# Key-value sums of a linear-attention block: one 128-column matmul for four heads, or four 32-column tiles

## The chip, the core and the metric

The kernel runs on one core of one Trainium2 chip. The metric is the device time of one execution in microseconds (us). Before the change it is 559.03 us, the median of three runs (558.52 to 559.60). All line numbers are those of the kernel before.

## The reference, cut to what matters

A block of linear attention with 32 heads of 32 channels is followed by an MLP over the tokens; x is 2048 tokens by 1024 channels, in bfloat16. The part at issue is `kv` and `z`:

```python
qkv = (layernorm(x) @ wqkv)                  # split in q, k, v; H = 32 heads, Dh = 32
phi = lambda t: where(t > 0, t + 1, exp(t)) + 1e-6
pq, pk = phi(q), phi(k)
kv  = einsum("bhsd,bhse->bhde", pk, v)       # 32x32 per head, summed over the 2048 tokens
z   = einsum("bhsd->bhd", pk)                # 32 per head
num = einsum("bhqd,bhde->bhqe", pq, kv)
den = einsum("bhqd,bhd->bhq", pq, z)[..., None] + 1e-6
o   = num / den
h   = x + o.reshape(B, S, D) @ wo
h2  = h + mlp_over_tokens(layernorm(layernorm(h)))   # S x F and F x S weights, F = 3584
```

Of each head's keys and values only the head's own 32x32 block of sums is wanted, and beside it the plain sum of its keys.

## The kernel before, in words

The 2048 tokens are 16 tiles of 128 (NS = 16), the 1024 channels 8 groups of 128 (ND = 8), so one group holds HB = 4 heads of DH = 32. The execution has three stages: up to about 143 us the layer norm, the projections to q, k and v and the key-value sums; up to about 230 us the folding of the sums into the output weights, the denominators and the attention's output; then the MLP over tokens, until the end at 557.7 us.

In the first stage keys and values of two token tiles at a time are computed by seven block products of 512 columns (class `Run`, lines 966 and following, with `KRun` and `VRun`); some of the queries (`q_unit`, line 1298; `QRun`, line 1103) are computed among them. Nearly every operation is pinned, so the order in the program text is the order on each engine. `run_step` writes that order out: of each run the products p1, p6, p2, p5, p7 and, inside the next run's step, p3 and p4.

The results go to two rings of four buffers each. `pks` holds phi of the keys of a token tile, 128 x 1024 bfloat16. `vaugs` holds the values, as 8 groups of 129 columns: 128 values and a one (line 814). The ones are filled in at the start (line 816). The values are written by ACT (line 903 for the first two tiles, line 1034 after that) and by DVE (line 1037, which adds two PSUM results).

`kv_accum(i)` (line 914) adds one token tile to the sums. For each group j of four heads it does one matmul on the full array: 128 tokens by the 128 key columns of the group are the stationary operand, the group's 129 value columns are the moving one, and 128 x 129 numbers are added in PSUM (line 917). All 16 cross products of four key heads with four value heads are computed, of which the four on the diagonal are wanted; column 129 is the sum of the keys. A PSUM bank holds three such groups (KPB = 3), so the eight groups take NKB = 3 banks (line 1281). The banks are cleared by DVE (line 1293), and the matmuls only ever accumulate (start=False). `kv_accum` is called for two token tiles at a time, eight times in all: after the first two products of the first value run (line 1322), behind p5 of the value runs (lines 1355, 1356), and at the end of the stage (lines 1377, 1378).

Behind the last call stand three more query units on TensorE (line 1379). Meanwhile DVE takes the sums out of PSUM: it multiplies each bank by a mask that holds 1/S on the four diagonal blocks and 0 elsewhere (`maskbd`, lines 105 to 110) into `kvbd` (line 1385), and spreads the key sums into `zz` (line 1391). `kv_transpose` (line 1418) then transposes kvbd on TensorE, and `den_mm` multiplies zz with the queries. `den_mm` is the one place where this kernel uses a part of the array: four matmuls of 32 stationary columns and 512 moving ones go to four column tiles (tile_position = (0, g * 32)) of one PSUM bank, for two sets of four groups.

Two other users are to be known: `warm_up` (line 98) does matmuls at the very start, among them two tiny ones whose operands are 128 x 6 and 128 x 2 float32; and `transpose_half` (line 1179) transposes in 128 x 128 blocks.

```python
        def kv_accum(i):                                  # line 914
            for j in range(ND):
                b, sl = divmod(j, KPB)
                pin(nc.tensor.matmul(
                    kv_ps[b][:, sl, :],
                    lhsT=pks[i % NPK][:, j * P:(j + 1) * P],
                    rhs=vaugs[i % NVA][:, j, :],
                    start=False, ...))
```

Of the kernel before, what the change touches and what calls it, by code (L numbers as in the profile page):

```python
# [10 lines left out]
P = 128  # L11
F32 = mybir.dt.float32
BF16 = mybir.dt.bfloat16
FP16 = mybir.dt.float16
ACT = mybir.ActivationFunctionType
ALU = mybir.AluOpType
# [5 lines left out]
DH = 32  # L22
BANK = 512
# [7 lines left out]
def kernel(  # L31
# [12 lines left out]
    nc = tc.nc  # L44
    x = A_x.flatten_outer_dims()
    o_dram = out.flatten_outer_dims()
    S, D = x.shape
    F = B_w1.shape[1]
    NS, ND, NF = S // P, D // P, F // P
    CW = min(BANK, D)  # L50
# [7 lines left out]
    JB = CW // P  # L58
    HB = P // DH
    QR = P // 4  # L60
    assert ND == 8 and 3 * HB <= QR
    KPB = BANK // (P + 1)
    NKB = (ND + KPB - 1) // KPB

    const = ctx.enter_context(tc.tile_pool(name="const", bufs=1))
    actx_psum = ExitStack()
# [18 lines left out]
    pin = tc.keep_in_program_order  # L85
# [16 lines left out]
        for t in range(n):  # L102
            mm(warm[:, 0:P], warm[:, 0:BANK])

    maskbd = const.tile([P, P], F32)
    nc.vector.memset(maskbd[:], 0.0)
    m4 = const.tile([P, HB], F32)
    nc.vector.memset(m4[:], 0.0)
    for q in range(HB):
        nc.vector.memset(maskbd[q * DH:(q + 1) * DH, q * DH:(q + 1) * DH], 1.0 / S)  # L110
        nc.vector.memset(m4[q * DH:(q + 1) * DH, q:q + 1], 1.0)
    eps_ln = const.tile([P, 1], F32)
    nc.vector.memset(eps_ln[:], LN_EPS)
# [70 lines left out]
    def phi_parts(dst, src, n, pool, view=lambda t: t, lean=False):  # L184
        e_sb = pool.tile([P, n], BF16, tag="phi_e", name="e_sb")
        r_sb = None if lean else pool.tile([P, n], BF16, tag="phi_r", name="r_sb")

        def act():
            pin(nc.scalar.activation(e_sb[:], src, ACT.Exp))  # L189
            if not lean:  # L190
                pin(nc.scalar.activation(r_sb[:], src, ACT.Relu))

        def dve():
            pin(nc.vector.tensor_scalar(e_sb[:], e_sb[:], 1.0, PHI_EPS, ALU.min, ALU.add))  # L194
            if lean:
                pin(nc.vector.scalar_tensor_tensor(dst, view(src), 0.0, view(e_sb[:]), ALU.max, ALU.add))
            else:
                pin(nc.vector.tensor_tensor(dst, view(e_sb[:]), view(r_sb[:]), ALU.add))

        return act, dve  # L200

    def phi_evac(dst, src, n, pool):
        for part in phi_parts(dst, src, n, pool):
            part()
# [222 lines left out]
    class Mixer1(Product7):  # L427
# [5 lines left out]
        def evac(self, fh, dh, ps, a=0, b=CW):  # L433
            ft = 2 * self.p + fh
            act.activation(
                (gE if fh == 0 else gO)[:, self.p, dh * CW + a:dh * CW + b],
                ps[:, a:b], ACT.Gelu_apprx_tanh, bias=b1_sb[:, ft:ft + 1], scale=1.0,
            )
# [74 lines left out]
    class Quad:  # L513
# [85 lines left out]
        def run2(self, rest, nxt, load, sums, cut):  # L599
# [38 lines left out]
            def third():  # L638
                self.in3 = Inner2(sts, 3, self.mov3, "i", self.add_to(e), None)
                shared(sts[0])  # L640
                evac(0, 0, self.t1)()
                self.in3.sums(slice(0, 2))

            self.interleave(in2, self.pieces(lambda st: st.p7_fill), {
                "b": every(lambda: sts[0].asum(3), sums[3]), "2": lambda: sts[1].asum(3),
                "7": lambda: load("p7"), "third": third,
                "end": lambda: self.late.append(evac(1, 0, self.t1)),
            }, (("7", None),))
            shared(sts[1])
# [9 lines left out]
            def begin_next():  # L659
                if nxt is not None:  # L660
                    nxt.in1 = nxt.inner(1)
                    nxt.in1.sums(slice(0, 2))
                evac(0, 1, e)()
# [119 lines left out]
    with ExitStack() as actx:  # L783
# [14 lines left out]
        kvbd = pqpool.tile([P, ND, P], BF16)  # L798
        zz = pqpool.tile([P, ND, QR + HB], BF16)
# [10 lines left out]
        with ExitStack() as a1:  # L810
            a1w = a1.enter_context(tc.tile_pool(name="a1w", bufs=1))
            wkv = a1w.tile([P, ND, 2 * D], BF16)
            NVA, NPK = 4, 4
            vaugs = [a1w.tile([P, ND, P + 1], BF16, name=f"vaug{t}") for t in range(NVA)]
            for t in range(NVA):
                nc.vector.memset(vaugs[t][:, :, P:P + 1], 1.0)
            pks = [a1w.tile([P, D], BF16, name=f"pk{t}") for t in range(NPK)]
            tv = [
                t.bitcast(FP16).rearrange("p (k c) -> p k c", c=CW)
# [59 lines left out]
            def ln_finish(i):  # L879
                xn, _, _, scale, norm, _, _ = ln.pop(i)  # L880
                for op in scale():
                    pin(op)
                pin(norm(slice(0, D)))
                nc.sync.dma_start_transpose(out=xnT[:, :, i * P:(i + 1) * P], in_=xn[:])
# [13 lines left out]
            def proj_evac(pp, i, c):  # L898
                if c < NDC:
                    phi_evac(pks[i % NPK][:, c * CW:(c + 1) * CW], pp[:, 0:CW], CW, a2k)  # L900
                else:
                    c2 = c - NDC
                    pin(nc.scalar.activation(
                        vaugs[i % NVA][:, c2 * JB:(c2 + 1) * JB, 0:P],
                        pp[:, 0:CW].rearrange("p (j e) -> p j e", e=P),
                        ACT.Copy,
                    ))

            def proj_unit(i, c, hold=None):
                pp = acc_tile()  # L910
                proj_mm(pp, i, c, range(ND), hold)
                proj_evac(pp, i, c)

            def kv_accum(i):
                for j in range(ND):
                    b, sl = divmod(j, KPB)
                    pin(nc.tensor.matmul(  # L917
                        kv_ps[b][:, sl, :],
                        lhsT=pks[i % NPK][:, j * P:(j + 1) * P],
                        rhs=vaugs[i % NVA][:, j, :],  # L920
                        start=False,
                        stop=(i == NS - 1),
                        skip_group_check=True,
                    ))

            hk2 = ND // 2

# [98 lines left out]
            class VRun(Run):  # L1026
# [1 line left out]
                    super().__init__(q, vmov)  # L1028

                def dst(self, h, c):  # L1030
                    return vaugs[(2 * self.q + h) % NVA][:, c * JB:(c + 1) * JB, 0:P]

                def evac(self, h, ps):
                    pin(nc.scalar.activation(self.dst(h, 0), ps[:].rearrange("p (j e) -> p j e", e=P), ACT.Copy))

                def add(self, h, ps):
                    pin(nc.vector.tensor_tensor(
                        self.dst(h, 1),
                        ps[:].rearrange("p (j e) -> p j e", e=P),
                        self.E[:].rearrange("p (j e) -> p j e", e=P),  # L1040
                        ALU.add,
                    ))

            class KRun(Run):
# [233 lines left out]
            less_acc()  # L1278
            vps = a1.enter_context(tc.tile_pool(name="vps", bufs=1, space=PSUM))
            kvp = a1.enter_context(tc.tile_pool(name="kvp", bufs=1, space=PSUM))  # L1280
            kv_ps = [kvp.tile([P, KPB, P + 1], F32, name=f"kvps{b}") for b in range(NKB)]
            proj_unit(0, NDC, pin)
            ln_finish(G0)
            w_sums(vmov, slice(0, 2))
# [4 lines left out]
            w_sums(vmov, slice(2, 4))  # L1289
            proj_unit(1, NDC + 1, pin)  # L1290
            ln_finish(G0 + 1)
            for b in range(NKB):
                nc.vector.memset(kv_ps[b][:], 0.0)

            def q_unit(u, j):
                qp = acc_tile()
# [23 lines left out]
            v1.p1()  # L1320
            q_fill()
            kv_accum(0)
            kv_accum(1)
            v1.p6()
            v1.p2()
# [11 lines left out]
            for q in range(2, NVP):  # L1337
# [3 lines left out]
                for n in runs:  # L1341
                    kind = type(n).__name__[0]
                    i = {"K": 2 * q + 3, "V": 2 * q + 4}.get(kind, NS)
                    if q == 5 and kind == "Q":
                        i = NS - 1 if n.half == 1 else NS
                    elif q == 6 and kind == "K":
                        i = NS
# [5 lines left out]
                    def after5():  # L1353
                        if kind == "V":
                            kv_accum(2 * q - 2)
                            kv_accum(2 * q - 1)
                        if i < NS:
                            ln_finish(i)
                            load_next(i + 2)
# [20 lines left out]
                q_fill()  # L1380
            nc.vector.memset(zz[:, :, 0:3 * HB], 0.0)
            nc.vector.memset(zz[:, :, 3 * HB:], float(S))
            for b in range(NKB):
                j0, n = b * KPB, min(KPB, ND - b * KPB)
                nc.vector.tensor_tensor(
                    kvbd[:, j0:j0 + n, :],
                    kv_ps[b][:, 0:n, 0:P],
                    maskbd[:].unsqueeze(1).to_broadcast([P, n, P]),
                    ALU.mult,
                )  # L1390
                nc.vector.tensor_tensor(
                    zz[:, j0:j0 + n, HB:2 * HB],
                    kv_ps[b][:, 0:n, P:P + 1].to_broadcast([P, n, HB]),
                    m4[:].unsqueeze(1).to_broadcast([P, n, HB]),
                    ALU.mult,
                )

        more_acc(3)
        warmctx.close()
# [441 lines left out]
```

## Time and profile before

| what | value |
|---|---|
| median of 3 runs | 559.03 us |
| span of the profiled execution | 557.7 us |
| TensorE busy in the span | 550.7 us (99%) |
| DVE busy | 443.8 us (80%) |
| ACT busy | 288.8 us (52%) |
| TensorE clock granted | 1.00 |
| matmuls of line 917 (128 x 129) | 128, 221 ns each |
| their weight loads (128 x 128) | 128, 98 ns each |
| first and last start of them | 33.2 and 137.6 us |

The span goes from the first to the last instruction of the one profiled execution. The profile has no other time for that execution; its span is 1.3 us under the median of the runs. Matmuls overlap: the record of one lasts longer than the distance to the next, so the distance between starts is the cost of a matmul in a row of them, and a busy TensorE is not TensorE at its peak. In the rows of the profile PE is TensorE's matmuls, PEld its weight loads, a row in order of time has its start, the time from its first start to its last end, the engine, the line, the operation, the tile that is written and those that are read, the shape, and the count. The chain that ended last is followed back from the last instruction: at each step to what released it or to the instruction ahead of it on its engine.

### The profile page before, as it was taken

The page shows a single profiled execution, that of the slowest core. Times are in us where ns is not written, and L with a number is a line of the kernel's source. Part 1 is how long each engine was busy: PE and PEld are TensorE (multiplying, and loading weights), DVE is VectorE, ACT ScalarE, POOL GpSimd, SP SyncE. Part 2 cuts the span into 40 slices and gives each one's busy share as a digit, 9 for nine tenths or more (in the row PEclk, how much of TensorE's full clock was granted, in tenths as well). Part 3 has the DMA queues.
Part 4 walks back from the last instruction along what each step waited for, and adds up shares of the span by engine and source line. Part 5 has one row for each costly group of instructions (what it writes and reads, how often), then busy time and mean ns, then how long its engine had stood idle before and what let it go on. Part 6 is the DMA issues. An engine that isn't in the chain of part 4 may idle for free.

```text
span 557.7 us, 8915 instructions
## 1 busy us (share of the span) xinstructions
PE 550.7 (99%) x3370; PEld 320.4 (57%) x3387; DVE 443.8 (80%) x858; ACT 288.8 (52%) x614; POOL 26.2 (5%) x36
## 2 busy tenths in 40 slices
PE   8999999999999999999999999999999999999997
PEld 3444446645444444456766767666444667667665
DVE  6898888754488688889989789887996879749747
ACT  5747678665776877646556465464210412413311
POOL 1000000000000000000000000000003103103111
PEclk9999999999999999999999999999999999999999
DMA  8933341202966961102250440413769659849434
GB/s 297 308 76 76 80 89 22 39 0 72 317 155 192 316 196 75 76 0 90 64 152 4 148 133 21 150 43 91 202 204 237 190 137 242 209 126 240 94 106 75
DMA packets 83931, 74.51 MB, mean 134 GB/s; under 512 B 15650, under 2 KB 76336, under 8 KB 83888
## 3 DMA queue, kind: packets, MB, share of 16 engines
q1 hardware_dynamic: 79504, 69.87, 42.0%
q0 software_dynamic: 4096, 3.68, 5.0%
q8 instruction: 26, 0.43, 0.3%
q10 hardware_dynamic: 288, 0.39, 0.2%
q14 instruction: 17, 0.14, 0.1%
HBM read 59.12 MB, written 11.67 MB: 127 GB/s over the span
## 4 chain that ended last, share of the span: by engine, by line
PE 91%; DMA 4%; DVE 2%; ACT 1%; SPq 1%; issue 0%; DVEq 0%; ACTq 0%
PE psI L234 23%; PE psC L234 14%; PE acc_t L234 14%; PE psB L234 8%; PE psC L966 4%; PE psB L966 4%; PE psA L966 4%; PE acc_t L888 3%; PE acc_t L1298 2%; PE psB L346 2%; PE psA L346 2%; PE psE L966 2%; PE psC L346 2%; DMA wq<-in_B_w_dram 2%; DMA wkv<-in_A_wqkv_dram 1%; PE kvps L917 1%
## 5 line engine op out<-in xcount | busy, mean ns | idle before, releaser
L234 PEld LDWEIGHTS <-is 128*128 128x128 f16 x736 | 71.8, 98 | 31.3 <-DVE is L234 0.4
L234 PEld LDWEIGHTS <-sa 128*128 128x128 f16 x606 | 59.2, 98 | 27.5 <-issue 0.3
L234 PEld LDWEIGHTS <-wq 128*128 128x128 bf16 (+1 forms) x496 | 48.5, 98 | 28.1 <-issue 1.2
L234 PE MATMUL acc_t<-wo_sb,pqT 128*128 128x512 f16 x256 | 55.6, 379 | 0.0
L491 POOL DMA_DIRECT2D out_dram<-wq x28 | 24.3, 927 | 519.6 <-ACT wq L494 487.7
L234 PEld LDWEIGHTS <-pqT 128*128 128x128 bf16 x256 | 25.0, 98 | 30.5 <-issue 0.6
L234 DVE TENSOR_TENSOR t<-psI,t 128x256 f32<-128x256 f32 (+1 forms) x45 | 20.8, 475 | 22.2 <-PE psI L234 21.0
L194 DVE TENSOR_SCALAR e_sb<-e_sb 128x512 bf16<-128x512 bf16 x64 | 18.4, 287 | 21.8 <-ACT e_sb L189 21.6
L234 PE MATMUL psC<-gs,wq 128*128 128x512 f16 x140 | 34.1, 379 | 0.0
L966 PEld LDWEIGHTS <-xs 128*128 128x128 f16 x208 | 20.1, 98 | 22.1 <-DVE xs L955 0.6
L234 PE MATMUL psC<-hT,sa 128*128 128x512 f16 x112 | 31.2, 379 | 0.0
L234 PE MATMUL psI<-hi,is 128*128 128x256 f16 x200 | 30.0, 273 | 0.0
L234 PE MATMUL psB<-hT,sa 128*128 128x512 f16 x112 | 29.7, 379 | 0.0
L234 PE MATMUL acc_t<-xnT,wq_sb 128*128 128x512 bf16 x125 | 29.3, 379 | 0.3
L189 ACT ACTIVATE e_sb<-acc_t 128x512 bf16<-128x512 f32 x32 | 19.1, 598 | 18.6 <-PE acc_t L1298 10.0
L234 DVE BATCH_NORM_STATS2 hst<-acc_t 128x6 f32<-128x512 f32 x32 | 21.4, 691 | 9.1 <-ACT h_bf L234 8.9
L966 PE MATMUL psA<-wkv,xnT 128*128 128x512 bf16 x98 | 26.2, 379 | 0.3
L966 PEld LDWEIGHTS <-xnT 128*128 128x128 bf16 x156 | 15.2, 98 | 18.1 <-issue 0.2
L234 PE MATMUL psC<-hT,wq 128*128 128x512 f16 x96 | 24.6, 379 | 0.0
L234 ACT CAST h_bf<-acc_t 128x512 bf16<-128x512 f32 x32 | 18.4, 582 | 12.0 <-PE acc_t L234 12.0
L234 DVE TENSOR_TENSOR e<-psI,es 128x256 f32<-128x256 f32 x20 | 8.5, 424 | 19.9 <-PE psI L234 19.9
L234 ACT COPY psI<-psI 128x256 f32<-128x256 f32 x50 | 18.0, 360 | 11.7 <-PE psI L234 9.8
(246 smaller groups left out, 1131.6 us busy)
## 6 DMA issues: line engine op xcount, KB each, us to landing
wq<-in_B_w_dram SPq DMA_DIRECT2D x14, 1024.0 KB, 7.9
wq<-in_B_w_dram SPq DMA_DIRECT2D x12, 896.0 KB, 7.6
gs<-parked SPq DMA_DIRECT2D x9, 896.0 KB, 4.7
shared_sb<-rd_dram SPq DMA_DIRECT2D x32, 128.0 KB, 3.9
out_dram<-h_bf SPq DMA_DIRECT2D x16, 256.0 KB, 2.0
x_sb<-in_A_x_dram SPq DMA_DIRECT2D x14, 256.0 KB, 3.0
w2o<-in_B_w_dram SPq DMA_DIRECT2D x4, 896.0 KB, 11.3
out_dram<-wq POOLq DMA_DIRECT2D x28, 128.0 KB, 4.6
```

The costliest lines, as they stand in the source:

```text
L189: pin(nc.scalar.activation(e_sb[:], src, ACT.Exp))
L194: pin(nc.vector.tensor_scalar(e_sb[:], e_sb[:], 1.0, PHI_EPS, ALU.min, ALU.add))
L234: return (lambda *a, **kw: pin(op(*a, **kw))) if self.always or getattr(Held, self.key) else op
L346: pe.matmul(ps[:, cols], lhsT=lhs[:, k, :], rhs=mv(k)[:, cols], start=(start and k == 0), stop=(k == self.nk - 1), skip_group_check=True,)
L491: nc.gpsimd.dma_start(to, ot[:, a:b], accum_op=ALU.add)
L888: mm = nc.tensor.matmul(pp[:, 0:CW], lhsT=xnT[:, kt, i * P:(i + 1) * P], rhs=wkv[:, kt, c * CW:(c + 1) * CW], start=(kt == 0), stop=(kt == ...
L917: pin(nc.tensor.matmul(kv_ps[b][:, sl, :], lhsT=pks[i % NPK][:, j * P:(j + 1) * P], rhs=vaugs[i % NVA][:, j, :], start=False, stop=(i == N ...
L966: pin(nc.tensor.matmul(ps[:], lhsT=lhs[:, k, :], rhs=rhs[:, k, :], start=(start and k == 0), stop=(k == hk2 - 1), skip_group_check=True,))
L1298: nc.tensor.matmul(qp[:, 0:SW], lhsT=wq_sb[:, kt, j * P:(j + 1) * P], rhs=xnT[:, kt, u * SW:(u + 1) * SW], start=(kt == 0), stop=(kt == ND ...
```

## The change

The sums are accumulated per head. For each group of four heads four matmuls are issued, head q of the group on column tile q: 128 tokens by the head's 32 key columns are stationary, the head's own 32 value columns and its one are moving, and 32 x 33 numbers are added at PSUM partitions 32q to 32q + 31. The 8 x 33 columns fit into one bank. The value buffers are laid out by head, 32 groups of 33 columns. The mask goes; kvbd is filled with zeros once, near the start of the program, and at the end four DVE operations copy the diagonal blocks, scaled by 1/S.

```diff
-            vaugs = [a1w.tile([P, ND, P + 1], BF16, name=f"vaug{t}") for t in range(NVA)]
+            vaugs = [a1w.tile([P, ND * HB, DH + 1], BF16, name=f"vaug{t}") for t in range(NVA)]
             for t in range(NVA):
-                nc.vector.memset(vaugs[t][:, :, P:P + 1], 1.0)
+                nc.vector.memset(vaugs[t][:, :, DH:DH + 1], 1.0)
+
+            def heads(t, c):
+                return t[:, c * JB * HB:(c + 1) * JB * HB, 0:DH]
+
+            def by_head(t):
+                return t.rearrange("p (h e) -> p h e", e=DH)
...
             def kv_accum(i):
                 for j in range(ND):
-                    b, sl = divmod(j, KPB)
-                    pin(nc.tensor.matmul(
-                        kv_ps[b][:, sl, :],
-                        lhsT=pks[i % NPK][:, j * P:(j + 1) * P],
-                        rhs=vaugs[i % NVA][:, j, :],
-                        start=False,
-                        stop=(i == NS - 1),
-                        skip_group_check=True,
-                    ))
+                    for q in range(HB):
+                        h = j * HB + q
+                        pin(nc.tensor.matmul(
+                            kv_ps[q * DH:(q + 1) * DH, j, :],
+                            lhsT=pks[i % NPK][:, h * DH:(h + 1) * DH],
+                            rhs=vaugs[i % NVA][:, h, :],
+                            start=False,
+                            stop=(i == NS - 1),
+                            skip_group_check=True,
+                            tile_position=(0, q * DH),
+                        ))
...
                 def evac(self, h, ps):
-                    pin(nc.scalar.activation(self.dst(h, 0), ps[:].rearrange("p (j e) -> p j e", e=P), ACT.Copy))
+                    pin(nc.scalar.activation(self.dst(h, 0), by_head(ps[:]), ACT.Copy))
...
-            kv_ps = [kvp.tile([P, KPB, P + 1], F32, name=f"kvps{b}") for b in range(NKB)]
+            kv_ps = kvp.tile([P, ND, DH + 1], F32, name="kvps")
...
-            for b in range(NKB):
-                nc.vector.memset(kv_ps[b][:], 0.0)
+            nc.vector.memset(kv_ps[:], 0.0)
+            nc.vector.memset(kvbd[:], 0.0)
...
-            for b in range(NKB):
-                j0, n = b * KPB, min(KPB, ND - b * KPB)
-                nc.vector.tensor_tensor(
-                    kvbd[:, j0:j0 + n, :],
-                    kv_ps[b][:, 0:n, 0:P],
-                    maskbd[:].unsqueeze(1).to_broadcast([P, n, P]),
-                    ALU.mult,
-                )
-                nc.vector.tensor_tensor(
-                    zz[:, j0:j0 + n, HB:2 * HB],
-                    kv_ps[b][:, 0:n, P:P + 1].to_broadcast([P, n, HB]),
-                    m4[:].unsqueeze(1).to_broadcast([P, n, HB]),
-                    ALU.mult,
-                )
+            for q in range(HB):
+                own = slice(q * DH, (q + 1) * DH)
+                nc.vector.tensor_scalar(kvbd[own, :, own], kv_ps[own, :, 0:DH], 1.0 / S, None, ALU.mult)
+            nc.vector.tensor_tensor(
+                zz[:, :, HB:2 * HB],
+                kv_ps[:, :, DH:DH + 1].to_broadcast([P, ND, HB]),
+                m4[:].unsqueeze(1).to_broadcast([P, ND, HB]),
+                ALU.mult,
+            )
```

Not shown are the removal of `maskbd` and of KPB and NKB, and the same change of view in the other writers of the value buffers (lines 903 and 1037). The order of all other instructions on TensorE, ACT, SP and POOL is the same.

More of the change, by code (lines that the diff above doesn't have):

```diff
@@ L61 @@
     assert ND == 8 and 3 * HB <= QR
-    KPB = BANK // (P + 1)
-    NKB = (ND + KPB - 1) // KPB
+    assert ND * (DH + 1) <= BANK
     const = ctx.enter_context(tc.tile_pool(name="const", bufs=1))
@@ L103, in warm_up @@
             mm(warm[:, 0:P], warm[:, 0:BANK])
-    maskbd = const.tile([P, P], F32)
-    nc.vector.memset(maskbd[:], 0.0)
     m4 = const.tile([P, HB], F32)
@@ L109 @@
     for q in range(HB):
-        nc.vector.memset(maskbd[q * DH:(q + 1) * DH, q * DH:(q + 1) * DH], 1.0 / S)
         nc.vector.memset(m4[q * DH:(q + 1) * DH, q:q + 1], 1.0)
@@ L903, in proj_evac @@
                     pin(nc.scalar.activation(
-                        vaugs[i % NVA][:, c2 * JB:(c2 + 1) * JB, 0:P],
-                        pp[:, 0:CW].rearrange("p (j e) -> p j e", e=P),
+                        heads(vaugs[i % NVA], c2),
+                        by_head(pp[:, 0:CW]),
                         ACT.Copy,
@@ L1030, in dst @@
                 def dst(self, h, c):
-                    return vaugs[(2 * self.q + h) % NVA][:, c * JB:(c + 1) * JB, 0:P]
+                    return heads(vaugs[(2 * self.q + h) % NVA], c)
                 def evac(self, h, ps):
-                    pin(nc.scalar.activation(self.dst(h, 0), ps[:].rearrange("p (j e) -> p j e", e=P), ACT.Copy))
+                    pin(nc.scalar.activation(self.dst(h, 0), by_head(ps[:]), ACT.Copy))
                 def add(self, h, ps):
                     pin(nc.vector.tensor_tensor(
[L1038 to L1041, printed above, removed]
+                        self.dst(h, 1), by_head(ps[:]), by_head(self.E[:]), ALU.add,
                     ))
```

## The prediction

> **What bounds the kernel now.** I read the busy shares first, then the chain of waits, then the instructions in order of time around the lines that the change touches. TensorE is busy for 550.7 of 557.7 us. The two lines tell the limit before any detail: no other engine comes near, and DVE's 443.8 us is spread under TensorE.
>
> ```profile
> span 557.7 us, 8915 instructions
> PE 550.7 (99%) x3370; PEld 320.4 (57%) x3387; DVE 443.8 (80%) x858; ACT 288.8 (52%) x614; POOL 26.2 (5%) x36
> PE 91%; DMA 4%; DVE 2%; ACT 1%; SPq 1%; issue 0%; DVEq 0%; ACTq 0%
> ```
>
> The last line is the chain that ended last: 91% of it is TensorE, so what the change adds to or takes from TensorE's queue goes to the end of the kernel nearly one to one. The chain between 30 and 150 us holds the key-value sums eight times, each time as a block of 16 matmuls (two token tiles). Three of the eight pieces (start, length):
>
> ```profile
> 33.38 0.94 PE kvps L917 x16
> ...
> 52.53 0.94 PE kvps L917 x16
> ...
> 136.90 0.94 PE kvps L917 x16
> ```
>
> The same block in order of time, with its neighbours (start, from first start to last end):
>
> ```profile
> 51.94 0.59 PE L966 MATMUL psE<-wo_sb,xs 128*128 128x512 f16 x2
> 52.37 1.11 PE L917 MATMUL kvps<-vaug,pk 128*128 128x129 bf16 x16
> 53.31 0.59 PE L966 MATMUL psC<-wo_sb,xs 128*128 128x512 f16 x2
> ```
>
> One matmul's record lasts 221 ns but they overlap: the next work starts 53.31 - 52.37 = 0.94 us later, so the pace is 0.94/16 = 59 ns for a weight load and a matmul. No wait stands before or behind the block. Eight blocks are 8 x 0.945 = 7.56 us of chain: the whole stake of the change.
>
> **What the new form costs, by the nearest rows.** The trace has one matmul in the new shape's column width: the denominators on zz, 128 rows by 32 columns, 512 moving columns, four tiles side by side.
>
> ```profile
> 144.38 0.81 PE L234 MATMUL acc_t<-xnT,wq_sb 128*128 128x512 bf16 x3
> 145.13 0.62 PE L234 MATMUL den_ps<-pqT,zz 128*32 128x512 bf16 x8
> 145.67 0.61 PE L234 MATMUL acc_t<-xnT,wq_sb 128*128 128x512 bf16 x2
> ```
>
> Two things are in it. First, the tiles do run side by side: eight matmuls of 512 columns take 0.62 us from first start to last end, where eight on the full array at 216 ns apart would take 7 x 0.216 + 0.38 = 1.89 us. A window of 0.06 us shows four of them started within 0.40 - 0.39 = some 0.01 us, so 3 to 4 ns apart:
>
> ```profile
> 145.13 0.40 PE L234 MATMUL den_ps<-pqT,zz 128*32 128x512 bf16 x4
> ```
>
> Second, changing the tile width costs time. The last full-width matmul before starts at 144.38 + 0.81 - 0.38 = 144.81; the next start should come 0.216 later and comes 0.31 later: 0.095 lost. The last wave on the tiles starts at 145.13 + 0.62 - 0.38 = 145.37 and the next full-width one at 145.67, again 0.31 less 0.216, 0.095 lost; the one behind that starts 0.227 later, 0.01 lost. In all **0.20 us per block**, 8 x 0.20 = 1.6 us, that the blocks of before do not pay.
>
> The rest is 64 weight loads and 64 matmuls of 33 columns per block instead of 16 and 16. No row has a long run of such small ones, so I bound their pace from both sides. The low end: four at a time and limited by columns alone, 59 x 33/129 = 15 ns for each of 16 groups of four, 0.24 us. The high end: each pair keeps the 59 ns at which the pairs of before come, 64 x 59 = 3.78 us. In between lie the only tiny matmuls of the trace, 6 and 2 columns:
>
> ```profile
> 5.03 0.20 PE L98 MATMUL acc_t<-st 128*6 128x6 f32 x2
> 5.48 0.19 PE L98 MATMUL acc_t<-mv 128*2 128x2 f32 x2
> ```
>
> One lasts 173 and 166 ns, so the second starts 27 to 31 ns behind the first, though there is next to nothing to stream: a pair costs some 29 ns on one tile. The open question is whether 29 ns is what one tile needs (then four tiles share it) or what TensorE needs to bring up the next pair in a run longer than it has ready. The 3 to 4 ns of zz speak for the first, but they are bursts of 8 to 16 instructions that stood ready behind the change of width; here 128 follow each other. The trace never shows TensorE take more than 32 instructions at under 30 ns each (the block of 16 pairs: 0.945 us/32). I take 29 ns for each of the 64 pairs, as the nearest row in size, and keep both ends.
>
> Sum for a block: 64 x 0.029 + 0.20 - 0.945 = +1.11 us. All eight: +8.9 us.
>
> What a notes page makes of it, beside those rows: the Trainium skill, TensorE: Matmul & The Clock Gate, section "Wait — 56ns, not 53.3ns?", says that starts never come closer than about 25 ns however few the columns, and that a sequencer that decodes in firmware needs about 62 ns per matmul. By the first figure my sum would be 8 x (1.60 + 0.20 - 0.945) = +6.8 us, by the second 8 x (3.97 + 0.20 - 0.945) = +25.8 us, estimates from that page. The 27 to 31 ns agree with the first; the 3 to 4 ns between different column tiles do not, for a burst. [...]
>
> **The other edits, none on the path.**
> - Value buffers by head (18 ACT writes on lines 903 and 1034, 600 ns each; 14 DVE adds on line 1037, 685 ns): same counts, runs of 32 numbers instead of 128. No row shows runs of 32. I take no change; between a loss of nothing and double, it would be 10.8 us more of ACT and 9.6 us more of DVE, where between 30 and 140 us ACT is busy 76.4 and DVE 85.6 of 110. Each add has the next two runs' matmuls, over 5 us, before its value block is read. Without that cover the 9.6 us would be the price; I give it 3%.
> - The end of the sums (lines 1385, 1391): six DVE operations, 2 x 0.54 + 0.41 + 3 x 0.155 = 1.96 us from 137.77 to 139.68, become four of 32 partitions x 256 and one of 128 x 32. Nearest row 0.41 for 256 columns: 4 x 0.41 + 0.16 = 1.8 us. The transposes that read them start at 142.86; three query units of TensorE, 5.2 us, cover it. Value nothing, between -0.1 and +0.1; without cover that is also what it would cost.
> - Clearing: three fills of 0.38 us at 22.5 to 25.4 become one of 264 columns (0.26), and the filling of kvbd comes in at the start, about 0.5 us by the same row, for five mask fills that go (0.17 + 4 x 0.09). DVE there idles 1.12 us for the first tile of x, and TensorE waits for neither: nothing.
> - The freed two PSUM banks are given to nobody; the order of the other TensorE work, ACT's, SP's and POOL's is the same, and no DMA moves. The first matmul of the sums keeps its wait for the clearing; the last fill of before starts at 25.4, the first matmul at 33.2.
>
> **The rivals.**
> 1. *The tiles carry it: faster.* If groups of four come at 29 ns (or at 15), a block is 16 x 0.029 + 0.20 = 0.66 us (0.44): 0.28 (0.50) saved, eight times -2.2 (-4.0) us: 556.8 (555.0). For it: 3 to 4 ns between tiles in the zz row, TensorE's later weight loads already issued while the first wave runs. Against it: never seen over more than 16 instructions. It decides when a pair comes up in under (0.945 - 0.20)/64 = 11.6 ns.
> 2. *TensorE is fed no faster than now: slower still.* At 59 ns a pair: 8 x (3.78 + 0.20 - 0.945) = +24.3 us, 583.3. For it: no run in the trace is denser. Against it: 59 ns at 129 columns can be the columns alone.
> 3. *Neither: within 0.2% (1.1 us).* Part of a block stands ready while the 512-column matmuls before it run, the rest comes at the slow pace; with 11.6 ns on average the two cancel. A narrow band between my case and rival 1.
> 4. *The change does not do what it says*, because four tiles on one bank wait for each other: then each pair costs one tile's 29 ns, which is my number again. The zz row, also four tiles on one bank, speaks against it.
>
> **How the numbers follow.** The profiled execution's span is 557.7 us, the median of the three runs 559.03; I keep the 1.3 us between them and add my sum to the median: 559.0 + 8.9 = **567.9 us**. Chances: my case and everything slower 56% (of it 13% above 579, near rival 2), rival 3 8%, rival 1 36%, almost all of it between 555.0 and 557.9. The range takes in rival 1 and leaves the far end of rival 2 out: 555.0 to 579.0. The likeliest case's own range is 562 to 574 (20 to 40 ns a pair: 8 x (1.28 + 0.20 - 0.945) = +4.3 to 8 x (2.56 + 0.20 - 0.945) = +14.5). 0.2% is about what a measurement of this kernel can tell from no change.
>
> **What will show it.** In the changed profile the sums should be 512 matmuls of 128*32, 33 columns, in eight places; the length of such a place, from its first start to the next full-width start, is the whole answer: about 2.1 us if I am right, 0.44 to 0.67 if the tiles carry it, 4.0 for rival 2, 0.945 for no change. An equal gap of 0.31 us on both sides should show the change of width. DVE's and ACT's rows for vaug should stay at 685 and 600 ns; a longer one, and TensorE idle behind it, would make me wrong for another reason, and so would any gap in TensorE outside these eight places.

## The result, and the profile after

The changed kernel takes 557.3 us (median of 12 runs, 556.87 to 558.55) beside 558.63 us for the kernel before (12 runs): ratio 0.9976, 95% interval 0.9967 to 0.9984. Timed again later, beside other runs of the kernel before, it gave 0.9966 (0.9952 to 0.9979). So it is faster by some 1.3 to 1.9 us, where I had forecast 8.9 us slower. The time went the way of rival 1.

Page of the changed kernel, the lines that answer to those shown of before:

```profile
span 555.3 us, 9676 instructions
PE 548.3 (99%) x3754; PEld 316.7 (57%) x3771; DVE 443.6 (80%) x851; ACT 289.0 (52%) x614; POOL 26.2 (5%) x36
PE 95%; DMA 2%; ACT 1%; DVE 1%; issue 1%; ACTq 0%; DVEq 0%
```

TensorE still bounds the kernel and is busy 2.4 us less, as much as the span is shorter; DVE and ACT are where they were. A profiled execution's time lies 1.75 us above its span here (557.03 and 555.3 for this one), so the first profile of before, with 557.7, was of an execution of 559.4 us, and its span is 0.4 to 0.8 us too long to be set against a median.

The chain of waits between 30 and 150 us, three of the eight places of the sums (start, length):

```profile
33.15 0.59 PE kvps L920 x64
...
52.07 0.59 PE kvps L920 x64
...
135.55 0.60 PE kvps L920 x64
```

and one place in order of time with its neighbours:

```profile
51.04 1.03 PE L970 MATMUL psE<-wo_sb,xs 128*128 128x512 f16 x4
52.00 0.66 PE L920 MATMUL kvps<-vaug,pk 128*32 128x33 bf16 x64
52.59 1.04 PE L970 MATMUL psC<-wo_sb,xs 128*128 128x512 f16 x4
```

The last full-width matmul ahead starts at 51.04 + 1.03 - 0.38 = 51.69, and 0.216 is its own due; the next full-width one starts at 52.59. The place costs 0.69 us (0.68 by these rounded numbers, 0.690 in the trace at each of the eight), and the start behind that one comes 0.01 late: 0.70, where it cost 0.945. The 64 matmuls themselves start within 0.66 - 0.18 = 0.48 us; the other 0.21 to 0.22 are the two changes of width. Inside, the starts of groups of four lie 25 ns apart for about the first 36 matmuls and 33 ns apart from then on, which is 8.3 ns a pair, or 4.2 ns for each of the 8 instructions of a group. On average a pair takes 7.6 ns: my estimate of 29 ns for every pair was almost four times too high.

Eight places at -0.245 are -1.96 us. The stage as a whole won less. From the weight load at 12.5 us, before which every profile scatters by some tenths of a us, to the first query load behind the last place, before takes 124.95 us in both of its profiles and the changed kernel 123.59 and 123.58: -1.36 us. The rest was given back in three of the eight places, behind token tiles 2 to 7. The first of them, TensorE and then DVE of the changed kernel:

```profile
54.33 1.03 PE L970 MATMUL psB<-wkv,xs 128*128 128x512 bf16 x4
55.39 1.02 PE L970 MATMUL psC<-wo_sb,xnT 128*128 128x512 f16 x4
```

```profile
54.19 0.55 DVE L869 TENSOR_SCALAR xn<-x_sb,mv,rstd 128x1024 bf16<-128x1024 bf16 x1
54.65 0.69 DVE L1041 TENSOR_TENSOR vaug<-psC,e 128x512 bf16<-128x512 f32 x1
```

p3 (psB) should be followed by p4 (psC) at 54.33 + 4 x 0.216 = 55.19; it starts at 55.39, right behind the end of DVE's add, 54.65 + 0.69 = 55.34. p4 accumulates onto the psC that this add reads. TensorE got there 0.2 us too early. In the kernel before the same two lines stand so:

```profile
55.04 1.03 PE L966 MATMUL psB<-wkv,xs 128*128 128x512 bf16 x4
55.90 1.03 PE L966 MATMUL psC<-wo_sb,xnT 128*128 128x512 f16 x4
```

There p4 follows p3 by 0.86 = 4 x 0.216: no wait, since the add ends at 55.12 + 0.68 = 55.80:

```profile
55.12 0.68 DVE L1037 TENSOR_TENSOR vaug<-psC,e 128x512 bf16<-128x512 f32 x1
```

So 0.195 us come back three times, 0.585 in all: -1.96 + 0.585 = -1.375, which agrees with the stage's -1.36 within 0.02.

### The profile page after: what moved, and what is told of

It is laid out like the page before. It is cut to its first block, busy times and chain, and to the rows that moved or that the text cites. A ratio compares the mean times of both kernels' runs of the same rounds, so it can differ in the third digit from the quotient of the medians.

```text
span 555.3 us, 9676 instructions
## 1 busy us (share of the span) xinstructions
PE 548.3 (99%) x3754; PEld 316.7 (57%) x3771; DVE 443.6 (80%) x851; ACT 289.0 (52%) x614; POOL 26.2 (5%) x36
## 4 chain that ended last, share of the span: by engine, by line
PE 95%; DMA 2%; ACT 1%; DVE 1%; issue 1%; ACTq 0%; DVEq 0%
PE psI L230 25%; PE psC L230 16%; PE acc_t L230 14%; PE psB L230 8%; PE psC L970 4%; PE psB L970 4%; PE psA L970 4%; PE acc_t L890 3%; PE acc_t L1299 2%; PE psB L342 2%; PE psA L342 2%; PE psE L970 2%; PE psC L342 2%; PE psA L230 1%; PE psE L342 1%; DMA rd_dram<-shared_sb 1%
## 5 line engine op out<-in xcount | busy, mean ns | idle before, releaser
L230 ACT COPY psI<-psI 128x256 f32<-128x256 f32 x50 | 18.0, 360 | 11.6 <-PE psI L230 9.8
```

The source lines that it names most:

```text
L230: return (lambda *a, **kw: pin(op(*a, **kw))) if self.always or getattr(Held, self.key) else op
```

## The experiments

Theory after the result: one column tile needs 25 to 29 ns for a pair and four tiles work side by side; from about the 36th pair on the coming of instructions sets the pace, 4.2 ns each; 0.2 us per place go to the changes of width; and DVE's add takes back 0.585 of the 1.96 us. Rivals are named in each expectation.

**e1_tile_by_tile**: neighbours on the same tile.

```diff
-                for j in range(ND):
-                    for q in range(HB):
+                for q in range(HB):
+                    for j in range(ND):
```

> The changed kernel with the two loops of the sums exchanged: for each column tile its eight groups one after the other, so that neighbouring matmuls share a tile and not four follow on four tiles. Same 64 pairs a place. Theory (29 ns is what one tile needs, four tiles share it): a place takes 64 x 25 to 29 ns + 0.20 = 1.80 to 2.06 us instead of 0.70, eight places +8.8 to +10.9 us against the changed kernel, some 566 to 568 us. Rival (the pace is set by how fast instructions come, whatever the tile): no change, some 557 us.

560.93 us beside 559.32, ratio 1.0026 (1.0014 to 1.0039).

```profile
51.76 1.03 PE L970 MATMUL psE<-wo_sb,xs 128*128 128x512 f16 x4
52.72 1.21 PE L920 MATMUL kvps<-vaug,pk 128*32 128x33 bf16 x64
53.86 1.04 PE L970 MATMUL psC<-wo_sb,xs 128*128 128x512 f16 x4
```

The same 64 matmuls start within 1.21 - 0.18 = 1.03 us, 16.4 ns apart on average, and a place costs 1.24 us. Both expectations miss: the order matters, so it is not the coming of instructions alone, and 1.24 is far from 1.80. But 16.4 ns is not what one tile needs. These are the starts on the first two tiles of this place, in ns from the first, from the trace's records sorted by tile:

```text
first tile:     0   39   64   89  114  139  164  189
second tile:  120  158  183  209  234  259  284  310
```

The trace does not name a matmul's tile. The sorting goes by the length of the records: in the changed kernel the first matmul on each tile lasts 190 to 192 ns and the next ones 177 to 179, and here such a long record comes every 120 ns. Sorted so, all 64 starts of each of the eight places lie within 5 ns of eight equal rows. By this reading one tile takes a pair every 25 ns, as the theory had it, and the next tile begins while three matmuls of the one before have yet to start, so that eight take 120 ns and not 200. The theory had left out this overlap. Even with it the order loses: 1.24 against 0.945, where the changed kernel has 0.69.

**e2_twice**: twice the instructions in a place, no more changes of width. Sums and key sums come out doubled, their ratio hardly changes.

```diff
-                            kv_accum(2 * q - 2)
-                            kv_accum(2 * q - 1)
+                            for t in (2 * q - 2, 2 * q - 1) * 2:
+                                kv_accum(t)
```

(and in the same way at the two ends of the stage)

> The changed kernel with each place's sums done twice (both kv and z come out doubled, their ratio is nearly the same). It adds 64 pairs to a place and no change of width. Theory (behind the first 36 pairs a pair comes every 8.3 ns): each place 0.53 us longer, 1.23 us, eight places +4.3 us, some 561.6 us. Rival (the run gets slower the longer it is, 29 ns a pair as I predicted, once nothing is left ready): +1.86 us a place, +14.8 us, some 572 us.

563.1 us beside 559.32, ratio 1.0068 (1.0049 to 1.0086).

```profile
52.39 1.20 PE L920 MATMUL kvps<-vaug,pk 128*32 128x33 bf16 x128
```

1.20 - 0.18 = 1.02 us for 128 matmuls against 0.48 for 64: the second 64 come at 8.4 ns a pair, and a place costs 1.225 us. That is the theory's number; there is no further slowing in a run of 256 instructions. The eight places are 4.28 us longer than the changed kernel's, the stage 3.70 (127.29 against 123.59): the three waits for DVE are gone, 0.58 us, because TensorE comes later again. The total is about 1.5 us longer than these explain; the trace has it in the last 90 us, where DVE waits up to 2.2 us for weights of the MLP. Why, is open.

**e3_split**: one token tile at a time, twice as many places.

```diff
                     def after5():
                         if kind == "V":
                             kv_accum(2 * q - 2)
-                            kv_accum(2 * q - 1)
...
                     def after7():
+                        if kind == "V":
+                            kv_accum(2 * q - 1)
```

(and in the same way at the two ends of the stage)

> The changed kernel with the two token tiles of each place apart: one behind p5, the other behind p7, so 16 places of 32 pairs. Theory (0.20 us for the two changes of width, and 32 pairs that stand ready come at 25 ns for four): a place 0.41 us, 16 of them 6.6 us instead of 8 x 0.70 = 5.6, +1.0 us before waits, some 558.3 us. Rival (the 0.20 is no price of the change of width but of the first loads, hidden when the run is short): 16 places of 0.25 us, 4.0 us, -1.6 us.

559.14 us beside 559.32, ratio 0.9996 (0.9981 to 1.0011). The theory's 558.3 beside 558.63 would be 0.9994.

```profile
52.34 0.38 PE L920 MATMUL kvps<-vaug,pk 128*32 128x33 bf16 x32
52.66 1.04 PE L970 MATMUL psC<-wo_sb,xs 128*128 128x512 f16 x4
53.62 0.38 PE L920 MATMUL kvps<-vaug,pk 128*32 128x33 bf16 x32
```

A place of 32 pairs costs 0.406 us, of which the starts take 0.20 and the changes of width the other 0.20. (At one of the 16 places the trace has four weight loads and three matmuls behind it, so a record is missing there, and the 0.23 us that it shows more are not a wait.) The sum is 16 x 0.406 = 6.5 us; theory 6.6. So the price of the changes of width is fixed, 0.2 us a place, however short the run. Eight more places cost 1.0 us net beside the changed kernel's 8 x 0.690 = 5.5, since the shorter runs start a little faster. The places are still 1.1 us shorter than before's 7.56, but the time can't be told from that of the kernel before: the interval reaches from 1.1 us less to 0.6 us more.

**e9_two_tiles_of_64**: two heads per matmul, half the instructions.

```diff
-                    for q in range(HB):
+                    for q in range(0, HB, 2):
                         h = j * HB + q
                         pin(nc.tensor.matmul(
-                            kv_ps[q * DH:(q + 1) * DH, j, :],
-                            lhsT=pks[i % NPK][:, h * DH:(h + 1) * DH],
-                            rhs=vaugs[i % NVA][:, h, :],
+                            kv_ps[j // KPB][q * DH:(q + 2) * DH, j % KPB, :, :],
+                            lhsT=pks[i % NPK][:, h * DH:(h + 2) * DH],
+                            rhs=vaugs[i % NVA][:, h:h + 2, :],
...
```

(and the two banks, their clearing and the copies at the end to match)

> The changed kernel on two column tiles of 64: two heads per matmul, 66 moving columns, 32 pairs a place, two PSUM banks. Half the instructions, the same changes of width. Theory (32 pairs stand ready, so columns alone set the pace: 66 columns, 30 ns for two): a place 16 x 0.030 + 0.20 = 0.68 us against 0.70, -0.2 us over eight. Rival (each pair has a price of its own of some 8 ns, as in the long run): 32 x 8.3 ns + 0.20 = 0.47 us, -1.9 us, some 555.5 us.

557.84 us beside 559.32, ratio 0.9972 (0.9960 to 0.9983), which can't be told from the changed kernel's.

```profile
52.24 0.70 PE L922 MATMUL kvps<-vaug,pk 128*64 128x66 bf16 x32
```

The 32 starts take 0.50 us, 32 ns for two side by side. A place costs 0.721, theory 0.68. Half the instructions do not help: a pair comes every 16 ns here, so the rival's 8.3 ns a pair is not what binds, and a tile of 64 with 66 columns needs 32 ns for a pair where a tile of 32 with 33 needs 25. Whether that is the moving columns or the wider weight load, no run separates.

**e11_half_columns**: the other half of that question. Half of each head's value columns is left out of the sums.

```diff
-                            kv_ps[q * DH:(q + 1) * DH, j, :],
+                            kv_ps[q * DH:(q + 1) * DH, j, DH // 2:],
...
-                            rhs=vaugs[i % NVA][:, h, :],
+                            rhs=vaugs[i % NVA][:, h, DH // 2:],
```

> The changed kernel with 17 moving columns in place of 33: half of each head's value columns is left out of the sums. Same instructions, same changes of width. Theory (in a place the instructions' coming sets the pace: 8 at 25 ns while they stand ready, then 4.2 ns each): a place stays at 0.69 us, at the least 0.66. Rival (columns set the pace): the 0.48 us of the place shrink towards half, a place of 0.45 us.

556.73 us (one execution; kernel before 558.97).

```profile
51.66 0.65 PE L920 MATMUL kvps<-vaug,pk 128*32 128x17 bf16 x64
```

A place costs 0.677 us, 0.013 less: halving the columns saves next to nothing. The groups of four start 25 ns apart at first and 33 ns later, as with 33 columns, so the columns set neither pace. In the second part one tile's own 25 ns do not bind either. What is left is the coming of instructions; that is an inference, since no run changed it alone.

**e8_full_width_by_head**: all of the change but the column tiles.

```diff
-                    for q in range(HB):
-                        h = j * HB + q
...
+                    b, sl = divmod(j, KPB)
                     pin(nc.tensor.matmul(
-                        kv_ps[q * DH:(q + 1) * DH, j, :],
-                        lhsT=pks[i % NPK][:, h * DH:(h + 1) * DH],
-                        rhs=vaugs[i % NVA][:, h, :],
+                        kv_ps[b][:, sl, :, :],
+                        lhsT=pks[i % NPK][:, j * P:(j + 1) * P],
+                        rhs=vaugs[i % NVA][:, j * HB:(j + 1) * HB, :],
...
```

(without `tile_position`, and with three banks, their clearing and the copies at the end to match)

> The changed kernel's buffers by head, fill of kvbd and copies at the end, but the sums on the full array again: 128 columns stationary, the group's 4 x 33 = 132 columns moving, three PSUM banks. Theory (all that moved the time is the column tiles): a place 16 x 60 ns = 0.96 us, the time of before, 558.6 to 558.8 us. Rival (the layout or the shorter clearing and copying carry a part of the gain): 557.3 to 558 us.

558.62 us beside 558.72, ratio 0.9989 (0.9978 to 1.0000).

```profile
51.99 1.10 PE L920 MATMUL kvps<-vaug,pk 128*128 128x132 bf16 x16
52.93 1.02 PE L969 MATMUL psC<-wo_sb,xs 128*128 128x512 f16 x4
```

A place costs 0.938 us, the stage 124.90 us against 124.95. Layout, clearing and copying carry none of the stage's gain.

**e4_norm_late**: DVE's add ahead of the normalize, in the changed kernel. In value runs `ln_finish` moves from behind the sums to behind p7 and the sums of x.

```diff
                     def after5():
-                        if i < NS:
+                        if i < NS and kind != "V":
                             ln_finish(i)
                             load_next(i + 2)
...
                     def after7():
+                        if i < NS and kind == "V":
+                            ln_finish(i)
+                            load_next(i + 2)
```

> The changed kernel with one move on DVE and ACT: in a value run's step the layer norm of a coming token tile (scale on ACT, normalize on DVE) stands behind the product p7's add and the sums of x, not ahead of them. Theory (in three of the eight places 0.195 of the 0.245 us won is given back, because p4 of that run waits for the add on DVE, which stands behind the normalize of 0.55 us): the three waits go, -0.59 us against the changed kernel, some 556.7 us, and the trace shows p4 start 0.216 us behind p3's last matmul. Rival (a wait of p6 for the sums of x or of ACT's copy takes its place): no change.

557.56 us, ratio 0.9967 (0.9954 to 0.9980).

```profile
55.33 1.03 PE L970 MATMUL psB<-wkv,xs 128*128 128x512 bf16 x4
56.19 1.03 PE L970 MATMUL psC<-wo_sb,xnT 128*128 128x512 f16 x4
```

p4 follows p3 by 0.86 us again: the wait is gone, in all three places, and the stage takes 123.01 us, 0.58 less than the changed kernel's. The time does not show it: 0.9967 stands beside 0.9966. This execution reached the point at 12.5 us one us later than the changed kernel.

**e4_norm_late_again**, to tell chance from a price:

> The late normalize once more, since its profile showed the three waits gone but its time no different from the changed kernel's, and its profiled execution had lost 0.8 to 1.2 us in the first 13 us. Theory (that loss is chance, the start is the same code): the start of this profile lies within 0.5 us of the others, span some 554.8 us. Rival (the move costs at the start what it wins later): the start is late again by 0.8 us or more.

557.52 us, ratio 0.9973 (0.9961 to 0.9986). The stage takes 123.02 us again. The start was late once more: the point at 12.5 us was reached at 13.2, after 13.5 in the first profile, where all other kernels' profiles have it between 12.2 and 12.9. That is 0.7 us behind the changed kernel's first profile and 0.9 behind its second, against the theory's 0.5 and the rival's 0.8, and the span is 555.6 us where the theory had 554.8. So the waits are gone for certain, but what that is worth in time is not shown by this kernel. Whether a late start belongs to it is open: e10, further down, holds the same move and reaches the point at 12.5.

**e5_norm_late_alone**: the same edit in the kernel before.

> The same move in the kernel before, without the change of the sums. Theory: p4 does not wait there (it starts 0.216 us behind p3), so nothing is gained, 558.6 us. Rival (the move is worth something by itself): some 558.0 us.

558.9 us beside 558.72, ratio 0.9999 (0.9987 to 1.0011); the stage takes 124.95 us, as without the edit. As the theory has it: the wait is a child of the faster sums.

**e10_norm_late_merged**: the same move, and one place fewer.

```diff
-                        if kind == "V":
+                        if kind == "V" and q + 1 < NVP:
                             kv_accum(2 * q - 2)
                             kv_accum(2 * q - 1)
...
-            kv_accum(NS - 2)
-            kv_accum(NS - 1)
+            for t in range(NS - 4, NS):
+                kv_accum(t)
```

> The changed kernel with the late normalize of the run before it, and with the sums of token tiles 12 and 13 moved to the end of the stage, so that the last place has four token tiles (128 pairs) and there are seven places. Theory: the three waits go (-0.59 us), and one place of 1.225 us stands for two of 0.690 (-0.155 us): some -0.7 us against the changed kernel, 0.9955 to 0.996 of the kernel before. Rival (the waits only move: DVE's own work sets the step): no better than the changed kernel, 0.997.

556.13 us (5 runs, 556.11 to 556.49), ratio 0.9947 (0.9932 to 0.9961). The last place:

```profile
134.19 1.20 PE L920 MATMUL kvps<-vaug,pk 128*32 128x33 bf16 x128
```

costs 1.224 us for 128 pairs where two of 0.690 stood, and the stage takes 122.85 us: 0.16 less than with the late normalize alone, 0.73 less than the changed kernel's, as the theory has it, and 2.10 less than before. It beats the kernel before clearly, and the changed kernel by some 1 us of median (556.13 against 557.3 and 557.11); its interval ends below that of the changed kernel's first timing (0.9961 against 0.9967) and overlaps that of the second (from 0.9952).

**after_again** and **before_again**: second profiles.

> The changed kernel itself, timed beside the others: 557.3 us, ratio 0.9976, and a second profile, in which each of the eight places again is 0.245 us shorter than before and three give 0.195 back. What differs between its two profiles is what one profile cannot tell.

> A second profile of the kernel before. The eight places are 0.945 us again. What differs from its first profile (start, the denominators' round trip around 150 us, a wait for weights around 512 us) is chance; if the wait at 512 us is there again and in none of the column-tile kernels, it belongs to the change.

The changed kernel, 557.11 us: the eight places 0.690 us each, three waits of 0.195 us, the stage 123.58 us, all as in its first profile. The kernel before: places of 0.945 us, stage 124.95 us; its span of 558.2 differs from the first in the last 50 us. There DVE waits for weights of the MLP, 0.49 us in the first and 1.08 us in the second profile (DVE of the first, in order of time):

```profile
511.52 0.62 DVE L234 TENSOR_TENSOR is<-wq 128x896 f16<-128x896 bf16 x1 [0.49 <-DMA wq<-in_B_w_dram]
```

and in e8 0.45 us, but not at all in the two profiles of the changed kernel. From one weight load a few us ahead of that wait to the end, the kernels on the full array (before twice, e5, e8) take 49.7 to 50.3 us, the changed kernel, e3, e4, e10 and e11 49.2, the slower e1 49.3, e9 49.4, and e2 51.5. So some 0.5 us or more of the difference in time between the two kernels may be this wait. It does not simply belong to the kernels on the full array: e2 has column tiles and waits there for 2.24 us. Nor does an earlier stage alone explain it, since e1 is later than before and does not have it. No run was made on it, and it stays open.

## Why the prediction was wrong, point by point

- **What bounds the kernel: right.** TensorE's chain, eight places of 0.945 us, and no other part of the change moved the stage: e8, with everything but the column tiles, is at the time of before.
- **The changes of width: right.** 0.20 us per place was read from the denominators' row; it measures 0.20 to 0.22 with 33 columns (e3, changed kernel), with the same 0.31 us between starts on the way in (52.00 - 51.69).
- **The pace of a pair: the step that failed.** "I take 29 ns for each of the 64 pairs, as the nearest row in size." In its place the runs show a pair every 6.2 ns among the first 36 and every 8.4 ns in a long run (e2), 0.48 us for the 64 where I had 1.86. The row's number was not bad as the need of one tile, which is 25 ns by my reading of e1 (the row's two records are one float32 call, so the closeness may be chance). The error was to charge it to every pair, as if TensorE and not one tile needed it: four tiles work through their 25 ns side by side. My low bound, 15 ns for a group by columns alone, was too low, since a group takes 25 ns with 33 columns and with 17 (e11). The measured 0.48 us lie just above rival 1's 0.24 to 0.46.
- **The open question** was put rightly, one tile's need or TensorE's, and I chose the wrong side. The zz row's 3 to 4 ns between tiles, which I set aside as a short burst, pointed the right way. A run longer than what stands ready does slow down, as I feared, but from 25 to 33 ns for a group of four, not to 116. Rival 1's condition, a pair in under 11.6 ns, is met at 8.4, with more than a quarter to spare.
- **The sum.** With 0.48 in place of 1.86 for the 64 pairs, my own sum gives 8 x (0.48 + 0.20 - 0.945) = -2.1 us, and the eight places measure -1.96. The formula was sound, one term was wrong. (A slip besides: the lower end of the likeliest case's range, 559.0 + 4.3, is 563.3 and not 562.)
- **The edits off the path: right but for one follow.** Value writes stayed at 600 and 686 ns, the end of the sums takes 1.9 us as before, the clearing moved nothing. What I wrote of slack, I wrote for a kernel that gets slower: for rival 1 I did not ask what TensorE would run into when it arrives 0.25 us earlier. It ran into DVE's add, which had had 0.1 us to spare (55.80 to 55.90), and lost 0.585 us. e4 shows it by taking the cause away, e5 that it was not there before.
- **The chances.** I gave the side that came 36%, and its own span, 555.0 to 557.9, held the result. That the time comes so near rival 1's 556.8 is partly luck: its sum had neither the 0.585 us lost to DVE's add nor the 0.5 us or so that the wait in the MLP may be worth.

A notes page and these runs: the Trainium skill, TensorE: Matmul & The Clock Gate, section "Wait — 56ns, not 53.3ns?", has starts no closer than about 25 ns, and some 62 ns per matmul where firmware decodes. As the pace of one column tile the 25 ns agree with e1; as a floor for TensorE they do not hold, with a matmul every 8.4 ns on four tiles in e2. The 62 ns do not bind in that row either; how the instructions are decoded here, no run shows. The Trainium skill, TensorEngine Tiling (Array Packing), section "Key Properties", says that a change of tiling mode drains TensorE; the 0.20 us per place fit that, though no run shows the drain itself.

## What to carry to other kernels

For small matmuls on column tiles, keep two paces apart: what one tile needs for a pair (here 25 ns, with 17 columns as with 33), divided by the tiles that work side by side, and what TensorE as a whole needs in a long run (here 8.4 ns a pair). The slower of the two counts. Before taking a row for either, ask which of the two it shows, and do not scale it down by columns without a row at that size. Column tiles pay for themselves only in places long enough to bear the 0.2 us of the two changes of width, so put such work together. And when a bound engine gets faster by 0.25 us, look at each of its next waits for one with less than that to spare.

## What the runs showed of the hardware that was not expected

- By the reading of e1, one tile of 32 columns takes a load and a matmul of 33 columns every 25 ns, and the next tile's first matmul starts at 120 ns, ahead of this tile's last three at 139 to 189. With 17 columns on four tiles the groups come no closer, 25 ns (e11).
- Four tiles together take a pair every 6.2 ns for about 36 pairs, and every 8.4 ns after that, over at least 128 pairs (e2). The 8.4 ns do not fall with half the columns (a place of 0.677 us for 0.690, e11).
- Two tiles of 64 with 66 columns take 32 ns for two pairs (e9).
- 132 moving columns on the full array cost no more than 129: 0.938 us against 0.945 for 16 (e8). Three columns more, and 7 ns less.
